# Top-k attention with a GELU block: reciprocals of the sums on POOL, and six more odd items turned by DVE and DRAM

## The chip, the cores and the metric

The kernel runs on one core of a Trainium2 chip. Its metric is the device time of one execution in microseconds (us); lower is better. Five engines work side by side, each through its own list of instructions in order, and they meet through semaphores: PE (matrix products, which also does transposes as products with an identity), DVE (vector work along a row), ACT (functions, and copies out of PSUM), POOL (vector work) and SP (which here only issues DMAs).

## The reference

There are 64 heads (batch 8 by 8 heads) with 576 rows and a head width of 64. For each head the scores are q times k transposed, times 1/8. In each row the 32 largest scores stay, a softmax is taken over those, and the result is multiplied with v. The outputs of the 8 heads of a batch are laid side by side into 512 columns, which gives 4608 rows, and these pass through two matrix products with an exact GELU between them.

```python
scores = scale * np.matmul(q, k.transpose(0, 1, 3, 2))
kth = np.partition(scores, -top_k, axis=-1)[..., -top_k:-top_k + 1]
scores = np.where(scores >= kth, scores, -1000000000.0)
attn = np.exp(scores - np.max(scores, axis=-1, keepdims=True))
attn = attn / (np.sum(attn, axis=-1, keepdims=True) + 1e-09)
x = bridge(np.matmul(attn, v))               # (4608, 512)
h = x @ w_in                                 # (4608, 2048)
out = (0.5 * h * (1.0 + erf(h / sqrt(2)))) @ w_out
```

## The kernel before

The work is cut into 144 items. An item is a tile of 128 rows for a pair of heads, and its tile `s` holds two rows of 576 scores side by side in each partition (128 x 1152). A batch has 18 items: 16 of full rows and two that collect the ends of the heads (64 rows each). Two batches make a round of 36 items (`RINGS`), and the program repeats with that period once the start is over.

The main loop (L1205) has one pass per item, here called slot n. All engines get their instructions in the order in which the loop writes them, so a slot is a stretch of each engine's list and not a stretch of time. What happens to item i, in order:

- Slot i-2: PE makes the scores (L408, and the last keys at L373), and ACT copies them to `s` (L416, L381). In slots of even number the scores of two items are made at once.
- End of slot i-2 to slot i-1: DVE takes the larger of the two halves of a row (L446, `larger`), and POOL their sum and then the smaller (L477, L485).
- Slot i: DVE finds the 32nd largest value of each row in `top_k` (eight MAX8 and six MATCH_REPLACE8). POOL then makes the threshold and the bias from it (L527, L528, `threshold`).
- Slot i+1: ACT pushes what is below the threshold far down (L547, `select`) and takes the exponential with the row's sum (L559, `softmax`). POOL adds 1e-9 to the sums (L540, `add_small`). At the end of `top_k` of that slot DVE takes the reciprocal of the two sums of each partition (L534, `inverse`), and POOL multiplies the tile with it (L582, `normalise`), behind the threshold of the next item.
- Slot i+2: the tile is turned so that keys lie along the partitions, in one of two ways. In the first, PE transposes it in nine pieces (one at L666, eight at L680) and ACT copies them from PSUM to the tile `pt` (L669, L695). In the second, DVE transposes squares of 32 x 32 in place (L614, `square_p`, in the middle of `top_k`), and SP writes the tile to DRAM (L624, `write_p`) and, a slot later, reads it back in another order into `pt` (L634, `read_p`).
- Slot i+3, when i is odd: PE multiplies `pt` of the items i-1 and i with v (L751, `attend`), ACT copies the result to `xT` (L756). `pt` exists once.

Which items take the second way is said by `squared`. These are, from item 27 on, nearly all items of even number, the items of ends, and those odd ones for which `moved` holds. An odd item that is moved has its product with v a slot later (slot i+4 in place of i+3), in the middle of the slot, with its own PSUM pair `pr`. The list `mid` in the main loop does that. `room_in` gives slot i+2 of such an item two pieces less of the matrix products of the second block, and slot i+3 two more.

The second block fills PE between these: first product (L820), GELU (L836), second product by seven products for eight (L974, L976), and the sums of it on POOL (L857 to L860, L997). In odd slots ACT copies one result of the second product out of PSUM (L995); the bank in which that result lies is the one into which PE next puts the last keys (L373).

`top_k` takes a function `last` that it calls behind the last MAX8: it issues `larger(n + 2)` and then `inverse(n - 1)`. A set `have_larger` keeps `larger` from being issued twice.

Of the kernel before, what the change touches and what calls it, by code (L numbers as in the profile page):

```python
# [14 lines left out]
def kernel(  # L15
# [19 lines left out]
    nc = tc.nc  # L35
    f32, i32, u32 = mybir.dt.float32, mybir.dt.int32, mybir.dt.uint32
    bf16, i16, u16 = mybir.dt.bfloat16, mybir.dt.int16, mybir.dt.uint16
    AF = mybir.ActivationFunctionType
    ALU = mybir.AluOpType

    B, H, S, D = q.shape
    P = 128
# [19 lines left out]
    const = ctx.enter_context(tc.tile_pool(name="const", bufs=1))  # L62
# [47 lines left out]
    def flush():  # L110
        held[0] = False
        while late_issues:
            late_issues.pop(0)()
        late_issues.extend(later)
        later.clear()
# [61 lines left out]
    DIAGS = START - 1  # L177
    SINGLE = range(18, 28)
    words = {}
    bounds = const.tile([P, 2], f32, name="bounds")  # L180
    low, high = bounds[:, 0:1], bounds[:, 1:2]
    nc.gpsimd.memset(low, -EXP0 * 2.0**20)
    nc.gpsimd.memset(high, EXP0 * 2.0**-40)

# [71 lines left out]
    for b in range(B):  # L258
# [4 lines left out]
        last = [(b * NP + p, NM) for p in range(0, NP, 2)]  # L263
# [8 lines left out]
    N = len(items)  # L272
# [4 lines left out]
    few = [False]  # L277
# [55 lines left out]
    S_of, stat_of = {}, {}  # L333
# [98 lines left out]
    def paired(i):  # L432

        return PAIRED <= i < N and i not in SINGLE

    def halves_of(i):
        s = S_of[i].rearrange("p (e h n) -> p e h n", e=2, h=2)
        return s[:, :, 0], s[:, :, 1]

    have_larger = set()  # L440

    def larger(i):

        if paired(i) and i not in have_larger:
            have_larger.add(i)
            nc.vector.tensor_tensor(lists_for(i)[:, :, 0], *halves_of(i), op=ALU.max)  # L446

    def into_of(i):

        if i < 2 and i not in into_lists:  # L450
            into_lists[i] = work.tile([P, 2, 2, HS], f32, tag="pt", bufs=1, name="into")
        return into_lists.get(i, lists_of[i])
# [13 lines left out]
    def lists_for(i):  # L466

        if i not in lists_of:
            lists_of[i] = work.tile([P, 2, 2, HS], f32, tag="lists", name="lists")
        return lists_of[i]  # L470
# [10 lines left out]
    def smaller(i):  # L481

        if paired(i):
            both, top = lists_of[i][:, :, 1].bitcast(i32), lists_of[i][:, :, 0].bitcast(i32)
            nc.gpsimd.tensor_tensor(into_of(i)[:, :, 1].bitcast(i32), both, top, op=ALU.subtract)  # L485

    def top_k(i, last, middle):


        stat_of[i] = st = {  # L490
            "first": work.tile([P, 2, 8], f32, tag="first", name="first"),
        }
        stat = work.tile([P, 4, 2], f32, tag="stat", name="stat")
        st.update((n, stat[:, x]) for x, n in enumerate(("neg", "bias", "den", "rden")))
        top = work.tile([P, 2, 16], f32, tag="top", bufs=1, name="top")
        into = [st["first"]] + [
            top[:, :, 8:16] if r == TOPK // 8 - 1 else top[:, :, 0:8] for r in range(1, TOPK // 8)
        ]
        if paired(i):
            t = lists_of[i]  # L500
            u = into_of(i)
            both = u.rearrange("p e h n -> p e (h n)")
            rounds = [(t[:, :, 0], u[:, :, 0]), (u[:, :, 0], u[:, :, 0])]
            rounds = [(*(rounds[r] if 16 * r < TOPK else (both, both)), x) for r, x in enumerate(into)]
        else:
            s = S_of[i].rearrange("p (e n) -> p e n", e=2)
            t = work.tile([P, 2, S], f32, tag="lists", name="rest")
            rounds = [(s if r == 0 else t, t, x) for r, x in enumerate(into)]
        for r, (src, dst, x) in enumerate(rounds):
            if 16 * r == TOPK:  # L510
                middle()
            for e in range(2):
                nc.vector.max(x[:, e], src[:, e])  # L513
            if r < len(rounds) - 1:
                for e in range(2):
                    nc.vector.match_replace(dst[:, e], x[:, e], src[:, e], LOWEST)  # L516
            if r == len(rounds) - 1:
                last()

        st["kth"] = top[:, :, 15]  # L520

    def threshold(i):

        if i < 0 or i >= N:
            return
        st = stat_of[i]
        nc.gpsimd.tensor_scalar(st["neg"], st["kth"], -1.0, None, op0=ALU.mult)  # L527
        nc.gpsimd.tensor_tensor(st["bias"], st["kth"], st["first"][:, :, 0], op=ALU.subtract)  # L528

    def inverse(i):  # L530
        if i < 0 or i >= N:
            return
        st = stat_of[i]
        nc.vector.reciprocal(st["rden"], st["den"])  # L534

    def add_small(i):
        if i < 0 or i >= N:
            return
        st = stat_of[i]
        nc.gpsimd.tensor_scalar(st["den"], st["den"], 1e-9, None, op0=ALU.add)  # L540

    def select(i, e):

        if i < 0 or i >= N:
            return
        st, s = stat_of[i], row(i, e)
        nc.scalar.activation(s, s, func=AF.Prelu, bias=st["neg"][:, e : e + 1], scale=1.0, alpha=STEEP)  # L547
        selected.add((i, e))
# [37 lines left out]
    def squared(i):  # L586

        if not SINGLE.stop - 2 < i < N - 2:
            return False
        if items[i][1] == NM:  # L590
            return i % RINGS != RINGS // 2 - 1
        return moved(i) or (i % 2 == 0 and i % RINGS != 12)

    LATER = (3, 13, 25, 31)

    def moved(i):

        return RINGS <= i < N - 8 and i % RINGS in LATER

# [10 lines left out]
    def square_p(i):  # L610

        if squared(i):
            s = S_of[i]
            nc.vector.transpose(s, s)  # L614

    def write_p(i):

        if squared(i):
            turned[i] = d = dram.tile([SQ, NJ + NM, P // SQ, P], f32, tag="turned", name="turned")
            s = S_of.pop(i).rearrange("p (x j) -> p x j", j=SQ)  # L620
            d = d.rearrange("i c k n -> i (c k) n")
            for a in range(P // SQ):
                rows = slice(a * SQ, (a + 1) * SQ)
                nc.sync.dma_start(out=d[:, :, rows], in_=s[rows])  # L624
# [498 lines left out]
    def mlp(n):  # L1123
        for _ in range(n):
            if done[0] >= len(pieces) or pieces[done[0]][0] > ready[0] or left[0] == 0:
                return
            pieces[done[0]][1]()
            done[0] += 1
            left[0] -= 1
            if eager[0]:  # L1130
                run_gelus()
                run_small(9)
# [72 lines left out]
    for n in range(ahead):  # L1205
# [27 lines left out]
        if n > 0:  # L1233
            larger(n + 1)
# [58 lines left out]
        if few[0]:  # L1293
            room = ODD if n % 2 else 0
            if mid and (mid[0] in starts_next or mid[0] % RINGS == LATER[0]):
                mlp(1)
# [34 lines left out]
            softmax(n - 1, 1)  # L1331
        if n > 0:
            smaller(n + 1)
        add_small(n - 1)
        for piece in tr[-1:] + prep:
            piece(None)
            mlp(1)
# [5 lines left out]
        mlp(left[0])  # L1343
        run_gelus()
        if n < N:
            def last():
                if few[0]:
                    larger(n + 2)
                inverse(n - 1)

            top_k(n, last, lambda: square_p(n - 2))
            write_p(n - 2)
            flush()
            if n == 0:
                larger(1)
        else:
            inverse(n - 1)
        threshold(n)
        if n == 0:
            smaller(1)  # L1360
# [60 lines left out]
```

## Time and profile before

| | |
|---|---|
| median of 3 runs | 1462.1 us (1461.39 to 1462.64) |
| the profiled execution | 1461.3 us, span 1459.5 us |
| PE busy | 1442.6 us, 99% of the span |
| DVE busy | 1329.6 us, 91% |
| POOL busy | 1128.4 us, 77% |
| ACT busy | 1056.4 us, 72% |
| DMA | mean 94 GB/s, 136.49 MB |

The span runs from the first instruction to the last. A row of a group of instructions has the line of the kernel, the engine, the operation, the tiles (out<-in), the shapes and the count; behind the bar stand the busy time of the group in us, the mean duration of one in ns, and the idle time of the engine just ahead of them with what ended it. Durations of matrix products overlap, since PE works on several at once. What one of them costs is therefore read from the start of one to the start of the next. PEld is the loading of PE's weights, which runs beside the products.

### The profile page before, as it was taken

The page shows a single profiled execution, that of the slowest core. Times are in us where ns is not written, and L with a number is a line of the kernel's source. Part 1 is how long each engine was busy: PE and PEld are TensorE (multiplying, and loading weights), DVE is VectorE, ACT ScalarE, POOL GpSimd, SP SyncE. Part 2 cuts the span into 40 slices and gives each one's busy share as a digit, 9 for nine tenths or more (in the row PEclk, how much of TensorE's full clock was granted, in tenths as well). Part 3 has the DMA queues.
Part 4 walks back from the last instruction along what each step waited for, and adds up shares of the span by engine and source line. Part 5 has one row for each costly group of instructions (what it writes and reads, how often), then busy time and mean ns, then how long its engine had stood idle before and what let it go on. Part 6 is the DMA issues. An engine that isn't in the chain of part 4 may idle for free.

```text
span 1459.5 us, 26550 instructions
## 1 busy us (share of the span) xinstructions
PE 1442.6 (99%) x8621; PEld 1123.9 (77%) x8621; DVE 1329.6 (91%) x3339; ACT 1056.4 (72%) x1883; POOL 1128.4 (77%) x1290
## 2 busy tenths in 40 slices
PE   8999999999999999999999999999999999999999
PEld 6776678877777777787777778787777777787887
DVE  7999999999999999999999999999999999999601
ACT  7999977777777777767777777777676767677620
POOL 6877657877798878878888878887788887878632
PEclk9999999999999999999999999999999999999999
DMA  7524310045454446456554365456554444543200
GB/s 196 150 87 126 84 48 1 9 98 104 90 113 89 87 87 142 82 113 128 111 99 96 65 117 116 90 112 127 117 102 106 90 80 84 127 98 85 53 15 15
DMA packets 591819, 136.49 MB, mean 94 GB/s; under 512 B 504352, under 2 KB 583232, under 8 KB 591680
## 3 DMA queue, kind: packets, MB, share of 16 engines
q1 hardware_dynamic: 590416, 134.37, 43.5%
q8 instruction: 68, 1.11, 0.3%
q14 instruction: 71, 0.58, 0.1%
q10 hardware_dynamic: 1200, 0.39, 0.1%
q0 software_dynamic: 64, 0.03, 0.0%
HBM read 85.19 MB, written 49.55 MB: 92 GB/s over the span
## 4 chain that ended last, share of the span: by engine, by line
PE 44%; POOL 11%; DVE 7%; issue 3%; ACT 3%; DMA 1%; SPq 0%; DVEq 0%; POOLq 0%; ACTq 0%
PE h_ps L820 17%; PE y_ps L976 11%; PE o L751 5%; PE s_ps L408 3%; POOL s L582 3%; DVE top L513 3%; DVE lists L516 2%; POOL lists L485 2%; POOL lists L477 2%; PE seven L974 2%; PE tp L680 2%; PE y_ps L938 2%; PE y_ps L941 1%; DMA turned<-s 1%; DVE s L614 1%
## 5 line engine op out<-in xcount | busy, mean ns | idle before, releaser
L820 PE MATMUL h_ps<-xT,w_in_sb 128*128 128x256 f32 (+1 forms) x2560 | 533.0, 361 | 0.0
L820 PEld LDWEIGHTS h_ps<-xT,w_in_sb 128*128 128x128 f32 x2560 | 438.9, 191 | 69.2 <-issue 10.9
L513 DVE MAX8 top<-lists 128x8 f32<-128x576 f32 (+1 forms) x792 | 475.9, 641 | 0.0
L547 ACT ACTIVATE s<-s,stat 128x576 f32<-128x576 f32 x288 | 219.2, 786 | 123.0 <-POOL stat L527 122.9
L516 DVE MATCH_REPLACE8 lists<-top,lists 128x288 f32<-128x288 f32 (+1 forms) x528 | 308.0, 589 | 0.0
L582 POOL TENSOR_TENSOR s<-s,stat 128x1152 f32<-128x1152 f32 x135 | 284.8, 2109 | 10.1 <-DVE stat L534 5.3
L559 ACT ACTIVATE s<-s,stat 128x576 f32<-128x576 f32 x288 | 225.2, 787 | 7.6
L485 POOL TENSOR_TENSOR lists<-lists 128x576 int32<-128x576 int32 x132 | 186.6, 1413 | 3.1
L477 POOL TENSOR_TENSOR lists<-s 128x576 int32<-128x576 int32 x133 | 188.2, 1415 | 0.0
L540 POOL TENSOR_SCALAR stat<-stat 128x2 f32<-128x2 f32 x144 | 44.4, 309 | 163.0 <-ACT s L559 156.1
L751 PE MATMUL o<-pt,raw_v 128*64 128x256 f32 x1280 | 152.9, 384 | 1.0 <-ACT pt L685 0.4
L416 ACT ACTIVATE s<-s_ps 128x1024 f32<-128x1024 f32 x127 | 126.4, 1046 | 35.2 <-PE s_ps L408 35.0
L751 PEld LDWEIGHTS o<-pt,raw_v 128*64 128x64 f32 x1280 | 86.8, 136 | 80.9 <-issue 38.1
L976 PE MATMUL y_ps<-w_out_sb,sum 128*128 128x256 f32 x472 | 140.4, 379 | 0.0
L408 PE MATMUL s_ps<-kt,qm 64*128 64x512 f32 x512 | 131.2, 621 | 1.1 <-ACT s L414 0.8
L836 ACT ACTIVATE g<-h_ps 128x512 f32<-128x512 f32 x144 | 78.2, 595 | 66.6 <-PE h_ps L820 66.0
L446 DVE TENSOR_TENSOR lists<-s 128x576 f32<-128x576 f32 x133 | 106.2, 799 | 17.8 <-ACT s L381 5.8
L976 PE MATMUL y_ps<-w_out_sb,g 128*128 128x256 f32 x480 | 116.4, 382 | 0.0
L516 DVE MATCH_REPLACE8 lists<-first,lists 128x288 f32<-128x288 f32 x264 | 114.4, 439 | 0.0
L513 DVE MAX8 first<-lists 128x8 f32<-128x288 f32 x268 | 105.8, 434 | 0.0
L976 PEld LDWEIGHTS y_ps<-w_out_sb,g 128*128 128x128 f32 x480 | 90.4, 190 | 15.0 <-issue 3.1
L976 PEld LDWEIGHTS y_ps<-w_out_sb,sum 128*128 128x128 f32 x472 | 89.8, 190 | 12.1
(162 smaller groups left out, 2359.0 us busy)
## 6 DMA issues: line engine op xcount, KB each, us to landing
turned<-s SPq DMA_DIRECT2D x272, 144.0 KB, 3.6
pt<-turned SPq DMA_DIRECT2D x272, 144.0 KB, 3.2
raw_v<-in_v_dram SPq DMA_DIRECT2D x64, 128.0 KB, 2.5
raw_q<-in_q_dram SPq DMA_DIRECT2D x112, 72.0 KB, 2.3
raw_k<-in_k_dram SPq DMA_DIRECT2D x112, 72.0 KB, 2.4
out_dram<-y SPq DMA_DIRECT2D x30, 256.0 KB, 3.1
w_out_sb<-in_moe_w_in_dram SPq DMA_DIRECT2D x14, 511.8 KB, 4.9
w_out_sb<-in_moe_w_out_dram SPq DMA_DIRECT2D x10, 511.8 KB, 4.1
```

Of the source, the lines that this page charges most:

```text
L408: nc.tensor.matmul(s_ps[:, e], lhsT=q_t[rows, :], rhs=kt[rows, main_keys(pair)], start=True, stop=True)
L416: nc.scalar.activation(spread(s, S + TL, SM), s_ps, func=AF.Copy, scale=scale)
L477: nc.gpsimd.tensor_tensor(t[:, :, 1].bitcast(i32), a.bitcast(i32), b.bitcast(i32), op=ALU.add)
L485: nc.gpsimd.tensor_tensor(into_of(i)[:, :, 1].bitcast(i32), both, top, op=ALU.subtract)
L513: nc.vector.max(x[:, e], src[:, e])
L516: nc.vector.match_replace(dst[:, e], x[:, e], src[:, e], LOWEST)
L547: nc.scalar.activation(s, s, func=AF.Prelu, bias=st["neg"][:, e : e + 1], scale=1.0, alpha=STEEP)
L559: nc.scalar.activation(s, s, func=AF.Exp, bias=st["bias"][:, e : e + 1], scale=1.0, accum_out=st["den"][:, e : e + 1],)
L582: nc.gpsimd.tensor_tensor(s, s, wide, op=ALU.mult)
L751: nc.tensor.matmul(o[e * D : (e + 1) * D, 0:n], lhsT=vt[:, j, e, :], rhs=pt[:, e * NJ + j if j < NM else NM, :], start=(j == 0), stop=(j = ...
L820: nc.tensor.matmul(h_tile(u)[:, i, :], lhsT=w_in_sb[:, ko, f * P : (f + 1) * P], rhs=xT[:, ko, c0 : c0 + n], start=(ko == 0), stop=(ko == ...
L976: nc.tensor.matmul(acc[names][:, k], lhsT=lhsT, rhs=rhs, start=(j == 0 and k == 0), stop=(j == FT // 2 - 1 and k == 1),)
```

## The change

The reciprocal leaves DVE. `inverse` now runs on POOL, takes in the addition of 1e-9 and raises the sum to the power -1 with a second small instruction, against a column of -1 that is set once. It is called where `add_small` stood, ahead of the threshold in POOL's list. `top_k` loses its argument `last`: `larger(n + 2)` isn't issued behind the last MAX8 any more but at the beginning of the next slot, as `larger(n + 1)` seen from there, which is the next thing in DVE's list all the same.

`LATER` gains the numbers 5 and 23. With the condition in `moved` (items 36 to 135) these are the items 41, 59, 77, 95, 113 and 131. They go from PE's transposes to DVE's squares with the way through DRAM, and their product with v moves from slot i+3 to the middle of slot i+4.

```diff
-    bounds = const.tile([P, 2], f32, name="bounds")
+    bounds = const.tile([P, 3], f32, name="bounds")
+    minus = bounds[:, 2:3]
...
+    nc.gpsimd.memset(minus, -1.0)
...
-    have_larger = set()
-
     def larger(i):
 
-        if paired(i) and i not in have_larger:
-            have_larger.add(i)
+        if paired(i):
             nc.vector.tensor_tensor(lists_for(i)[:, :, 0], *halves_of(i), op=ALU.max)
...
-    def top_k(i, last, middle):
+    def top_k(i, middle):
...
-            if r == len(rounds) - 1:
-                last()
...
         st = stat_of[i]
-        nc.vector.reciprocal(st["rden"], st["den"])
-
-    def add_small(i):
-        if i < 0 or i >= N:
-            return
-        st = stat_of[i]
         nc.gpsimd.tensor_scalar(st["den"], st["den"], 1e-9, None, op0=ALU.add)
+        nc.gpsimd.tensor_tensor(
+            st["rden"], st["den"],
+            bass.AP(tensor=minus.tensor, offset=minus.offset, ap=[list(minus.ap[0]), [0, 2]]),
+            op=ALU.pow,
+        )
...
-    LATER = (3, 13, 25, 31)
+    LATER = (3, 5, 13, 23, 25, 31)
...
-        add_small(n - 1)
+        inverse(n - 1)
...
-            def last():
-                if few[0]:
-                    larger(n + 2)
-                inverse(n - 1)
-
-            top_k(n, last, lambda: square_p(n - 2))
+            top_k(n, lambda: square_p(n - 2))
...
-        else:
-            inverse(n - 1)
```

## Prediction

> **What bounds the kernel now.** First the page: busy times, and DVE in 40 slices.
>
> ```profile
> PE 1442.6 (99%) x8621; PEld 1123.9 (77%) x8621; DVE 1329.6 (91%) x3339; ACT 1056.4 (72%) x1883; POOL 1128.4 (77%) x1290
> DVE  7999999999999999999999999999999999999601
> ```
>
> PE is busy throughout, and DVE nearly so until the last 80 us. The view by stretches shows both in the steady part (us, then busy time and instructions of PE, PEld, DVE, ACT, POOL). The first row is the start, the next two are rounds of 36 slots, the last is the tail.
>
> ```profile
> 0.00:111.40 111.40, 100.85 (x741) 79.89 (x743) 101.83 (x279) 99.62 (x171) 83.65 (x93) 1.00 0.49 142
> ...
> 695.80:1037.80 342.00, 341.01 (x2014) 266.06 (x2012) 332.98 (x839) 249.08 (x450) 283.51 (x323) 1.00 0.52 105
> 1037.80:1380.00 342.20, 341.54 (x2031) 266.90 (x2027) 325.95 (x827) 250.10 (x452) 282.37 (x324) 1.00 0.46 94
> 1380.00:1459.50 79.50, 75.66 (x368) 65.35 (x366) 4.90 (x12) 14.78 (x32) 23.65 (x33) 0.99 0.04 14
> ```
>
> A round takes 342.0 us, 9.5 per slot. PE is idle for 1.0 us of it, DVE for 9.0, POOL for 58.5, which is 1.62 per slot. That PE is truly full is read from starts (start, us, engine, line):
>
> ```profile
> 784.85 0.27 PE L666 MATMUL tp_t<-ident,s 128*128 128x128 f32 x1
> 784.96 0.60 PE L976 MATMUL y_ps<-w_sum,sum 128*128 128x256 f32 x2
> ...
> 785.82 1.04 PE L680 MATMUL tp<-ident,s 128*128 128x128 f32 x8
> 786.70 0.60 PE L976 MATMUL y_ps<-w_sum,g 128*128 128x256 f32 x2
> 787.13 0.59 PE L976 MATMUL y_ps<-w_out_sb,sum 128*128 128x256 f32 x2
> 787.66 1.99 PE L408 MATMUL s_ps<-kt,qm 64*128 64x512 f32 x8
> ```
>
> Two products of 256 columns take 0.43 us from start to start, and eight transposes of 128 columns 0.88: 0.9 ns per column both times, with no hole between kinds. The Trainium skill (Perfetto Trace Analysis, Identifying the Most-Contended Engine) says that matmul busy time is a poor measure of how full PE is, and asks for LDWEIGHTS busy time; that is 266 of 342 us here, and by that rule a fifth would be free and taking products away would be worth little. The starts above show no such room, and other rows show waits only at a few spots (below), so I keep PE as the bound and give the rule's outcome a place among the rivals.
>
> So PE sets the end, DVE has 3% of slack, and the two lean on each other through POOL and ACT.
>
> **The change part by part.** Rows of groups (busy us, mean ns | idle before), and of two small POOL instructions min/median/max ns:
>
> ```profile
> L680 PE MATMUL tp<-ident,s 128*128 128x128 f32 x536 | 69.6, 273 | 0.0
> L666 PE MATMUL tp_t<-ident,s 128*128 128x128 f32 x67 | 18.8, 281 | 0.0
> L695 ACT COPY pt<-tp 128x1024 f32<-128x1024 f32 x65 | 66.3, 1020 | 34.9 <-PE tp L680 34.6
> L669 ACT COPY pt<-tp_t 128x128 f32<-128x128 f32 x76 | 21.4, 282 | 4.2 <-PE tp_t L666 4.2
> L614 DVE STREAM_TRANSPOSE s<-s 128x1152 f32<-128x1152 f32 x68 | 92.8, 1365 | 0.0
> L534 DVE RECIPROCAL stat<-stat 128x2 f32<-128x2 f32 x144 | 22.7, 158 | 31.1 <-POOL stat L540 27.8
> L528 POOL TENSOR_TENSOR stat<-top,first 128x2 f32<-128x2 f32 x144 | 55.9, 388 | 0.0
> ...
> L540 POOL TENSOR_SCALAR stat<-stat x144: 217/218/833, 26.2 to 1381.8; 128x2 f32<-128x2 f32 x144
> L527 POOL TENSOR_SCALAR stat<-top x144: 218/218/1312, 18.2 to 1375.7; 128x2 f32<-128x2 f32 x144
> ```
>
> *PE, transposes away.* Six items lose nine transposes each: 0.88 + 0.11 (784.85 to 784.96) = 0.99 us, six times: **-5.9**. The two pieces that `room_in` moves between slots i+2 and i+3 are the same work.
>
> *PE, the product with v moved.* Before, it follows the scores directly. In its new place it stands alone between full-height products. A change of shape costs about 0.1 us (787.13 to 787.66 is 0.53, against 0.43 without one), and there is one such change more: 6 x 0.1 = **+0.6**.
>
> *ACT* loses 1.02 + 0.28 us per item, 7.8 in all. It is 72% busy: 0 on the path, and its relief comes behind the waits priced below.
>
> *DVE* loses 144 x 158 ns = 22.7 us and up to 31.1 us of waits for POOL's sum, and gains 6 x 1.365 = 8.2. The net is 14.5 or more off. DVE isn't the bound, so 0 directly; what it gives is an earlier end of `top_k`. `larger` keeps its place in DVE's list: 0, covered by the same neighbours.
>
> *DMA.* Each item adds four writes, four reads on SP's queue:
>
> ```profile
> turned<-s SPq DMA_DIRECT2D x272, 144.0 KB, 3.6
> pt<-turned SPq DMA_DIRECT2D x272, 144.0 KB, 3.2
> ```
>
> The 6.8 us from square to `pt` stand against the slot and a half, some 14 us, that the moved product leaves. Each read waits on SP for its write to land, and the loads and the next write queued behind it wait too, 3.6 us at most. Cost 0; if that cover is gone PE waits for `pt`.
>
> *POOL, the power.* No row has one. From below, a POOL instruction on 128x2 takes at least 0.217 us (L540's shortest); from above I use 1.31, the longest that one of this size took (L527's). Nearest is L528, also with two inputs of 128x2: mean 0.39. With 0.08 of hand-over from L540 to L527 (798.74 to 798.82 below) I take p = 0.47, ends 0.30 and 1.39. On average it is covered by the 1.62 us per slot of idle POOL. But it stands ahead of the threshold, and ACT waits for that, in one round:
>
> ```profile
> ACT s L547 <- POOL stat L527: 39.8, 13, 6.2
> POOL stat L540 <- ACT s L559: 33.4, 14, 4.3
> DVE stat L534 <- POOL stat L540: 3.5, 4, 1.0
> PEld s_ps L408 <- ACT pt L695: 2.7, 6, 0.9
> ```
>
> Behind the waiting ACT the chain goes on to PE. All engines, in slots 82 and 83:
>
> ```profile
> 797.90 0.77 DVE L446 TENSOR_TENSOR lists<-s 128x576 f32<-128x576 f32 x1
> 798.13 0.61 POOL L540 TENSOR_SCALAR stat<-stat 128x2 f32<-128x2 f32 x1
> ...
> 798.82 0.22 POOL L527 TENSOR_SCALAR stat<-top 128x2 f32<-128x2 f32 x1
> ...
> 799.07 1.44 ACT L547 ACTIVATE s<-s,stat 128x576 f32<-128x576 f32 x2 [3.80 <-POOL stat L527]
> ...
> 802.79 0.38 ACT L995 COPY p<-seven 128x256 f32<-128x256 f32 x1
> ...
> 803.43 0.39 PE L373 MATMUL tp_t<-kt,qm 128*128 128x128 f32 x2
> ```
>
> ACT selects, loads the GELU's table, runs two GELUs, and only then frees at 803.17 the bank that PE fills at 803.43: 0.26 us to spare. The same pair in slots 75, 79 and 97:
>
> ```profile
> 728.03 0.38 ACT L995 COPY p<-seven 128x256 f32<-128x256 f32 x1
> 728.66 0.38 PE L373 MATMUL tp_t<-kt,qm 128*128 128x128 f32 x2
> ...
> 765.28 0.38 ACT L995 COPY p<-seven 128x256 f32<-128x256 f32 x1
> 765.79 0.41 PE L373 MATMUL tp_t<-kt,qm 128*128 128x128 f32 x2
> ...
> 937.83 0.38 ACT L995 COPY p<-seven 128x256 f32<-128x256 f32 x1
> 938.26 0.49 PE L373 MATMUL tp_t<-kt,qm 128*128 128x128 f32 x2 [0.32 <-ACT p L995]
> ```
>
> Room of 0.25, 0.13 and none (PE waits already), mean of the four 0.16. These recur each round: 12 spots, 12 x (0.47 - 0.16) = 3.7 us if nothing comes earlier. Against that DVE's list is shorter by 0.16 us per slot and by its waits, so thresholds come earlier relative to PE; but POOL and not DVE is late in such slots (L540 begins 0.23 behind L446). I take half: **+1.8**, ends 0 and 12 x 1.23 = 14.8.
>
> The same rows show something else: L540 takes 0.61 beside L446 and ends 0.07 behind it, where its median is 0.22. The Trainium skill (SBUF — State Buffer, Who interferes with whom) states that a VectorE instruction with two SBUF inputs and a GpSimd one that reads SBUF exclude each other, the later one waiting; the trace agrees. By that rule a power that starts in L446's shadow costs up to 0.77 in place of 0.39, and one that starts ahead of L446 holds DVE up.
>
> *Start.* In the first slots POOL's multiplied diagonals come p later; ACT is the fuller engine there (99.62 of 111.40 us, with the loading of the first data in it) and I count 0. Without that cover it is about two slots, 0.9.
>
> Sum against the profiled execution: 1461.3 - 5.9 + 0.6 + 1.8 = 1457.8. That execution lies 0.8 below the median of the runs, so the forecast is **1458.6**, 3.5 us or 0.24% faster. A difference under 0.2% (2.9 us) is about what a measurement can't tell from none.
>
> **The rivals.**
>
> *B, no lateness.* DVE's freed time covers the power, and PE's idle time in the steady part (1.0 and 0.7 us in the rounds shown, another 0.7 taken for the first) goes too: 1458.6 - 1.8 - 2.4 = 1454.4. For it: DVE waited for POOL's sum (3.5 per round), and this ends. Against: POOL's own lateness.
>
> *C, the power's delay reaches PE (the slower side).* Place: the 12 spots. Price 12 x (p - 0.16) with no relief. The 5.3 us gained are gone at p = 0.60; slower by 0.2% from p = 0.84. With L540's longest, 0.83 + 0.08 = 0.91, it is 1462.1 - 5.3 + 9.0 = 1465.8. At p = 1.39: 1471.6. For it: ACT's 39.8 us of waits for L527. Against: a power as long as a multiplication.
>
> *D, a power far above all rows.* Beyond 1.62 us per slot POOL is the bound: at 3 us, 36 x 1.4 = 50 per round, three rounds: about 1610. No row speaks for it; none excludes it.
>
> *F, the squares make DVE late.* In slots 7 and 25 of a round DVE gets 1.37 longer just where PE gets shorter; two odd slots on, PE has 0.26 to spare. 6 x (1.37 - 0.26) = 6.7 eats the gain: 1462.1 - 5.3 + 6.7 = 1463.5. That is what the rule on matmul busy time comes to here: products taken off PE return as waits. Against: four reciprocals less (0.63) ahead of that spot.
>
> *E, the change doesn't do what it says:* `pt` comes late for the moved products, with waits of 0.9 us each (the 5.3 over six) the gain is lost: 1462.1.
>
> **How the numbers follow.** Forecast 0.45 (1456.5 to 1460.5), B 0.15, C 0.15, F 0.12, D 0.08, E 0.05. The range reaches down to B less the unpaid 0.6, 1453.5, and up to C at p = 0.91, 1466; outside stay D, C's upper part and a little of E. Faster by over 0.2% (below 1459.2): B and three quarters of the forecast, 0.5. Slower (above 1465): D, half of C, some of F: 0.2. Within: 0.3.
>
> **What would show it.** L680 x488, L666 x61, L614 x74, L534 gone, and a POOL row of 144 powers whose mean is p. ACT's wait for L527 grows by p in the slots with that wait; PE's waits at L373 for L995 tell C from B. If L446 waits for ACT more, DVE has run ahead. A power of over 1 us, or waits of PE behind the new squares, would make the forecast wrong.

## The result and the profile after

The changed kernel takes 1483.29 us (median, 1482.55 to 1483.7), the kernel before 1461.92 us beside it. The ratio is 1.0145 with a 95% interval of 1.013 to 1.0161: 21.4 us slower, where 3.5 us faster was forecast and 1466 was the upper end of the range.

First the page of the changed kernel: span, busy times, and POOL's 40 slices.

```profile
span 1481.8 us, 26751 instructions
PE 1446.2 (98%) x8567; PEld 1116.9 (75%) x8567; DVE 1340.7 (90%) x3201; ACT 1050.7 (71%) x1871; POOL 1219.1 (82%) x1435
POOL 6888668978898889888898989998888988988732
```

No engine is fuller than before except POOL, which went from 77% to 82%. A loss of 21 us with every share below 99% has to be sought in waits.

The groups that the change touches show that it was made as described (line, engine, operation, tiles, shapes, count; busy us, mean ns; idle before):

```profile
L676 PE MATMUL tp<-ident,s 128*128 128x128 f32 x488 | 63.7, 273 | 3.6 <-ACT xT L752 3.6
L610 DVE STREAM_TRANSPOSE s<-s 128x1152 f32<-128x1152 f32 x74 | 101.6, 1373 | 9.3 <-POOL s L578 9.3
L532 POOL TENSOR_TENSOR stat<-stat,bounds 128x2 f32<-128x2 f32 x144 | 108.1, 750 | 12.0
L531 POOL TENSOR_SCALAR stat<-stat 128x2 f32<-128x2 f32 x144 | 52.8, 367 | 151.8 <-ACT s L555 145.0
L445 DVE TENSOR_TENSOR lists<-s 128x576 f32<-128x576 f32 x133 | 122.1, 919 | 29.8 <-ACT s L383 18.2 <-ACT s L394 1.0
```

48 of the big transposes (and six of the small ones) have left PE, six squares have come to DVE, and the reciprocal is gone. The power (L532) takes 0.75 us in the mean and 0.72 in the median, with 12.0 / 144 = 0.08 us of hand-over ahead of it. `larger` is L445 now (L446 before). Its mean was 799 ns and is 919, with the same work.

The waits of the whole trace (who waited <- for whom; us, times, longest):

```profile
ACT s L543 <- POOL stat L524: 170.8, 54, 6.7
DVE lists L445 <- ACT s L383: 18.2, 23, 2.2
DVE top L512 <- POOL stat L525: 11.2, 16, 1.8
PE t_ps L375 <- ACT p L991: 10.4, 9, 1.6
PE tp_t L375 <- ACT p L991: 5.0, 10, 0.7
```

Before, the first of these was 122.9 us in 45 waits; DVE's wait for POOL's bias (L525, which must read the one buffer of `top` before the next MAX8 writes there) did not exist, and PE's waits for that copy came to 1.0 us in three. PE waits at the kind of spot that the forecast had looked at, the last keys (L375 now) for ACT's copy of the bank (L991). These two rows are 15.4 us; PE's time without work went from 16.9 us of the span to 35.6.

Stretches of four slots show where this comes from (us; busy time and instructions of PE, PEld, DVE, ACT, POOL). Three of them of the kernel before, and then, behind a whole round, the same slots of the changed kernel:

```profile
733.12:769.82 36.70, 36.66 (x195) 28.12 (x191) 36.07 (x93) 26.94 (x49) 34.21 (x40) 1.00 0.53 112
886.43:924.25 37.82, 37.56 (x315) 30.61 (x313) 36.28 (x93) 26.84 (x49) 34.10 (x41) 1.00 0.65 140
924.25:961.19 36.94, 36.62 (x224) 28.65 (x221) 36.28 (x93) 28.07 (x52) 30.93 (x36) 1.00 0.40 78
```

```profile
703.65:1052.90 349.25, 342.14 (x1999) 263.07 (x1998) 338.01 (x805) 247.02 (x446) 306.29 (x359) 1.00 0.55 109
742.13:781.01 38.88, 37.35 (x189) 27.20 (x186) 37.92 (x89) 27.51 (x49) 36.95 (x45) 1.00 0.54 104
898.78:937.51 38.73, 38.13 (x317) 30.72 (x315) 37.32 (x88) 27.43 (x51) 36.82 (x44) 1.00 0.64 135
937.51:976.83 39.32, 37.21 (x219) 27.97 (x216) 37.93 (x90) 26.34 (x50) 33.87 (x41) 1.00 0.52 103
```

The first row of the second fence is a whole round: 349.25 us against 342.0. Three rounds with some 7 us more each make nearly the whole loss. In the first stretch POOL had 36.70 - 34.21 = 2.49 us free over four slots, 0.62 per slot. The round's mean, on which the forecast leaned, was 1.62. Four powers with hand-over are 4 x 0.80 = 3.2 us: they do not fit, and the stretch has grown by 2.18 us.

The share over four slots doesn't tell the whole, though. The stretch that grew most, by 2.38 us, is the third, where POOL had 6.01 us free and still has 5.45; the first two together make 3.1 of the round's 7.2 us. Most of POOL's idle time is waiting for ACT and PE, and much of it stayed: over the round POOL got 22.8 us more to do, its idle time fell by only 15.5, and the round grew by 7.2. Taken slot by slot (from DVE's first MAX8 of one slot to that of the next), POOL had under 0.8 us free in 14 of the 36 slots, two of them, with 0.24 each, in the third stretch. Why the growth lies behind some of these slots and not behind others isn't settled: another stretch, in which POOL had 5.63 us free, got 1.03 us shorter.

One slot of the first stretch from POOL to PE, first before, then after (start, us, engine, line; other rows are left out, and the forecast showed the last two steps of before):

```profile
759.15 1.42 POOL L485 TENSOR_TENSOR lists<-lists 128x576 int32<-128x576 int32 x1
760.65 0.22 POOL L540 TENSOR_SCALAR stat<-stat 128x2 f32<-128x2 f32 x1
760.69 0.76 DVE L446 TENSOR_TENSOR lists<-s 128x576 f32<-128x576 f32 x1
760.95 0.58 POOL L527 TENSOR_SCALAR stat<-top 128x2 f32<-128x2 f32 x1
761.56 1.44 ACT L547 ACTIVATE s<-s,stat 128x576 f32<-128x576 f32 x2 [6.15 <-POOL stat L527]
```

```profile
769.42 1.41 POOL L484 TENSOR_TENSOR lists<-lists 128x576 int32<-128x576 int32 x1
770.12 1.32 DVE L445 TENSOR_TENSOR lists<-s 128x576 f32<-128x576 f32 x1
770.92 0.61 POOL L531 TENSOR_SCALAR stat<-stat 128x2 f32<-128x2 f32 x1
771.61 0.71 POOL L532 TENSOR_TENSOR stat<-stat,bounds 128x2 f32<-128x2 f32 x1
772.29 0.23 POOL L524 TENSOR_SCALAR stat<-top 128x2 f32<-128x2 f32 x1
772.56 1.44 ACT L543 ACTIVATE s<-s,stat 128x576 f32<-128x576 f32 x2 [6.74 <-POOL stat L524]
...
776.28 0.38 ACT L991 COPY p<-seven 128x256 f32<-128x256 f32 x1
776.72 0.49 PE L375 MATMUL t_ps<-kt,qm 128*128 128x128 f32 x2 [1.39 <-ACT p L991]
```

From the start of POOL's last big instruction (L485, now L484) to ACT's select went 2.41 us before and 3.14 after, 0.73 more. The room in this slot was 0.13 us by the forecast; a wait of 1.39 needs 1.52, so about 0.8 us of lateness had been brought along from the slots before, where POOL was full too. The rows show a second thing. `larger` now starts while POOL's L484 runs, takes 1.32 in place of 0.76 and ends at 771.44, 0.61 behind L484's end.

### The profile page after: what moved, and what is told of

Its sections match the earlier page's. It is cut to its first block, busy times and chain, and to the rows that moved or that the text cites. A ratio compares the mean times of both kernels' runs of the same rounds, so it can differ in the third digit from the quotient of the medians.

```text
span 1481.8 us, 26751 instructions
## 1 busy us (share of the span) xinstructions
PE 1446.2 (98%) x8567; PEld 1116.9 (75%) x8567; DVE 1340.7 (90%) x3201; ACT 1050.7 (71%) x1871; POOL 1219.1 (82%) x1435
## 4 chain that ended last, share of the span: by engine, by line
PE 62%; POOL 15%; ACT 10%; DVE 5%; issue 3%; DMA 2%; SPq 1%; ACTq 0%; DVEq 0%; POOLq 0%
PE h_ps L816 23%; PE y_ps L972 12%; PE o L747 6%; PE s_ps L410 5%; PE tp L676 3%; POOL s L578 3%; ACT s L543 2%; DVE top L512 2%; POOL lists L484 2%; PE y_ps L934 2%; PE y_ps L916 2%; PE seven L970 2%; PE y_ps L937 2%; POOL lists L476 2%; ACT L832 2%
## 5 line engine op out<-in xcount | busy, mean ns | idle before, releaser
L484 POOL TENSOR_TENSOR lists<-lists 128x576 int32<-128x576 int32 x132 | 190.6, 1444 | 3.1
L531 POOL TENSOR_SCALAR stat<-stat 128x2 f32<-128x2 f32 x144 | 52.8, 367 | 151.8 <-ACT s L555 145.0
L445 DVE TENSOR_TENSOR lists<-s 128x576 f32<-128x576 f32 x133 | 122.1, 919 | 29.8 <-ACT s L383 18.2
L532 POOL TENSOR_TENSOR stat<-stat,bounds 128x2 f32<-128x2 f32 x144 | 108.1, 750 | 12.0
L610 DVE STREAM_TRANSPOSE s<-s 128x1152 f32<-128x1152 f32 x74 | 101.6, 1373 | 9.3 <-POOL s L578 9.3
```

## The experiments

The theory at first: the power stands ahead of the threshold, so every threshold is late by it (rival C of the forecast). Rivals: POOL's time counts wherever it stands; the six items are the loss (rival F); the freed DVE time is what does harm; the power, which reads two inputs from SBUF, holds up DVE's `larger`. The first four runs take the change apart. All times are medians in us, beside 1461.8 to 1461.9 for the kernel before.

**The power alone.** `LATER` stays as before.

```diff
-    LATER = (3, 5, 13, 23, 25, 31)
+    LATER = (3, 13, 25, 31)
```

> The changed kernel with LATER as before (3, 13, 25, 31): only the reciprocal's move is left. Theory 1 (the power, 0.72 us with its hand-over 0.08, stands ahead of the threshold and delays it, then ACT's selection, then PE at L373): the whole loss is here, and the six items give back some 5 us of PE's transposes; expects 1483 to 1489 us. Theory 2 (the six squares make DVE late, the power is mostly covered): expects 1463 to 1468 us.

Measured 1479.38, ratio 1.012 (1.0105 to 1.0135): 17.5 us. The power by itself makes most of the loss, and the wait of PE at the last keys is there without the items:

```profile
PE tp_t L375 <- ACT p L991: 12.2, 16, 1.6
```

**The items alone.** The kernel before with the new `LATER`.

> The kernel before with LATER as changed (3, 5, 13, 23, 25, 31): the reciprocal stays on DVE, the six items go by squares and DRAM. Theory 1: faster than before by up to the 5.3 us of the forecast's PE terms, 1457 to 1461 us. Theory 2: most of the loss is here, 1475 us or more. A third way: DVE, which keeps the reciprocals, has no room for 8.2 us of squares, and the time stays within 2 us of 1462.

Measured 1467.97, ratio 1.0042 (1.0027 to 1.0056): 6.1 us slower, where the transposes taken off PE should have given 5.3. A round of this kernel, and two of its waits:

```profile
697.96:1042.24 344.28, 340.88 (x1998) 263.55 (x1996) 335.77 (x841) 246.96 (x446) 283.10 (x323) 1.00 0.56 111
```

```profile
PE tp L680 <- ACT xT L756: 3.7, 6, 1.0
PE o L751 <- DMA pt<-turned: 1.1, 1, 1.1
```

The round is 2.3 us longer than before. DVE's busy time rose from 333.0 to 335.8, which is the two squares of 1.37, while its idle time stayed at 8.5 us (9.0 before): the round grew by about what DVE had to do more. PE's idle time rose from 1.0 to 3.4 us; the work taken off it came back as waits, in the next odd slot behind the square (L373 and L680) and once for `pt`. The first row is a cost of the moved product itself. Its result lies in the one PSUM pair into which PE next puts the transposes (both take it by `pair_tile`), and these wait until ACT has copied the result (L756): 0.98 us behind each of the three new items of number 5, and 0.25 behind the three old ones of number 25. In the kernel before, PE has no such wait. That PE's busy time did not fall in spite of 18 transposes less is not resolved further by the trace.

**A multiplication in place of the power**, in the changed kernel.

```diff
-            op=ALU.pow,
+            op=ALU.mult,
```

> The changed kernel with a multiplication in place of the power, on the same operands and in the same place: POOL's list, the waits and the six items are those of the changed kernel, only the length of that instruction falls, from 0.72 to about 0.2 us. It leaves the reciprocal out. Theory 1 expects the loss to go with the length: 1457 to 1463 us. Theory 2 expects 1475 us or more. If the place of one more POOL instruction counts, whatever its length, it stays above 1470.

Measured 1466.3, ratio 1.0031 (1.0019 to 1.0043). The 17 us between this kernel and the changed one hang on what the second instruction takes on POOL, 0.26 us or 0.75 in the mean. They don't hang on `larger`:

```profile
L445 DVE TENSOR_TENSOR lists<-s 128x576 f32<-128x576 f32 x133 | 124.1, 934 | 21.9 <-ACT s L383 7.8 <-ACT s L394 2.5 <-DVE top L512 0.5
```

Its mean is 934 ns with the multiplication and 919 with the power, so a power that holds up `larger` isn't where the 17 us come from.

**The power behind the threshold**, called between the threshold of item n and the normalisation of item n-1.

```diff
         nc.gpsimd.tensor_scalar(st["den"], st["den"], 1e-9, None, op0=ALU.add)
+
+    def power(i):
...
         nc.gpsimd.tensor_tensor(
             st["rden"], st["den"],
...
+        power(n - 1)
         normalise(n - 1)
```

> The changed kernel with the power behind the threshold and the bias of the next item, just ahead of the normalisation; the addition of 1e-9 stays in its place. POOL's work is the same. Theory 1 (what counts is what stands ahead of the threshold): most of the loss goes, 1458 to 1468 us, less what a later normalisation costs. A rival to it (POOL as a whole is too full, 0.8 us more per slot wherever it stands): within 4 us of 1483.

Measured 1483.49, ratio 1.015 (1.0133 to 1.0167), the same as the changed kernel. So the place ahead of the threshold isn't the cause, and the first theory fell. POOL's list in this run:

```profile
769.67 0.22 POOL L524 TENSOR_SCALAR stat<-top 128x2 f32<-128x2 f32 x1
769.86 0.20 POOL L525 TENSOR_TENSOR stat<-top,first 128x2 f32<-128x2 f32 x1
770.01 0.72 POOL L537 TENSOR_TENSOR stat<-stat,bounds 128x2 f32<-128x2 f32 x1
770.80 2.11 POOL L583 TENSOR_TENSOR s<-s,stat 128x1152 f32<-128x1152 f32 x1
```

The threshold is out before the power, but normalisation and everything behind it start later by the power, and so does the next threshold: in a full stretch POOL hands the delay on.

**Less of other work on POOL**, with the power alone (the first experiment), in 16 slots per round one difference of 0.73 us less.

```diff
-        add(a21, a11, a21, op=ALU.subtract)
+        if u == NU - 2:
+            add(a21, a11, a21, op=ALU.subtract)
```

> The power-only kernel (LATER as before) without one of the four sums that POOL makes for the seven products (the difference a11 - a21, 0.73 us, 16 times in a round): it leaves that difference out. POOL is relieved by 11.7 of the some 29 us per round that the power brought, while the power stays where it is. Theory A expects a third to two thirds of the loss to go, 1466 to 1473 us. Theory B expects 1477 to 1480.

Measured 1464.0, ratio 1.0014 (1.0005 to 1.0024): 15.4 of the 17.5 us come back, with the power still in its place and as long as before. What counts is POOL's time, whichever instruction takes it.

**No addition of 1e-9**, in the changed kernel: POOL is relieved by one small instruction per item. The sum holds the exponential of the largest value, so it is at least 1, and 1e-9 is less than half a last place of it.

```diff
-        nc.gpsimd.tensor_scalar(st["den"], st["den"], 1e-9, None, op0=ALU.add)
```

> The changed kernel without the addition of 1e-9 (the sum holds an exponential of 0, so it is at least 1 and the addition changes no bit of it): POOL is relieved by 0.22 us and a hand-over of 0.08 per slot, the power stays. If POOL's slack ends between 0.6 and 0.8 us, most of the 21 us goes, 1464 to 1472 us. If the power's own reading is the cause, 1478 to 1483.

Measured 1468.27, ratio 1.0044 (1.0029 to 1.0059). An instruction whose median is 0.22 us and mean 0.37 brings 15.0 us, since it goes from a full POOL. It also ran beside `larger` often, as the slot above shows (0.61 in place of 0.22).

**No reciprocal**, in the kernel before and with the new items. This separates DVE's relief from POOL's load.

```diff
-        nc.vector.reciprocal(st["rden"], st["den"])
```

> The kernel before without any reciprocal, as in the run of the items without it: LATER as before, normalisation multiplies with the sums, which leaves the reciprocal out. It shows the most that the reciprocal's move can bring. If PE alone is the bound, as forecast, 1461 to 1462 us. If DVE bounds as much as PE does, 1452 to 1458.

> The kernel with the six items alone (1468.0) without any reciprocal: normalisation multiplies with the sums themselves, which leaves the reciprocal out. DVE loses 144 small instructions and its waits for POOL's sums, POOL's list is that of before. If the items cost because DVE is full (its list longer by 2.7 us per round, the round by 2.3), the time falls to 1456 to 1463. If they cost at fixed places (the copy of the moved product, the reload of pt), it stays at 1465 to 1468.

Measured 1463.75 without the reciprocal, ratio 1.0013 (1.0004 to 1.0022), and 1464.34 with the items beside it, ratio 1.0017 (1.0008 to 1.0027). Taking 22.7 us of busy time from DVE makes the kernel 1.8 us slower when nothing else is changed. `larger` in one round, before and then without the reciprocal:

```profile
L446 DVE TENSOR_TENSOR lists<-s 128x576 f32<-128x576 f32 x36 | 28.7, 796 | 4.4 <-ACT s L381 0.8
```

```profile
L446 DVE TENSOR_TENSOR lists<-s 128x576 f32<-128x576 f32 x36 | 33.4, 928 | 5.8 <-ACT s L381 2.2 <-ACT s L392 0.5
```

DVE comes to `larger` earlier and meets a large instruction of POOL more often: 9 of 36 take over 0.9 us (eight beside L485, one beside the normalisation), where 3 did. This gives back 4.7 us per round. The reciprocal itself was worth less than its 158 ns: outside such meetings the step from the start of `larger` to that of the next MAX8 got shorter by 0.08 to 0.10 us. That the meetings are the whole of the 1.8 us is argued, not shown by a run. With the items there, the reciprocal's removal does help: 1467.97 without it removed, 1464.34 with, which falls between the two readings that the expectation had set apart. So the items cost 6.1 us with the reciprocal on DVE and 0.6 without it.

**Memsets and multiplications where the power stood**, with the old items, the reciprocal left out and the sum itself taken by the normalisation: how much POOL time costs how much, and whether the power does anything else.

```diff
-        nc.gpsimd.tensor_tensor(
-            st["rden"], st["den"],
-            bass.AP(tensor=minus.tensor, offset=minus.offset, ap=[list(minus.ap[0]), [0, 2]]),
-            op=ALU.pow,
-        )
+        for x in range(9):
+            nc.gpsimd.memset(bounds[:, 2 + x % 6 : 3 + x % 6], -1.0)
```

This is the run with nine. Six and 22 differ in the number, and the run with multiplications has this in place of the memsets:

```diff
+        for x in range(4):
+            nc.gpsimd.tensor_tensor(bounds[:, 6:8], bounds[:, 2:4], bounds[:, 4:6], op=ALU.mult)
```

> The power-only kernel (LATER as before) with six memsets of one column each in place of the power: POOL is held for about 0.6 us at the same place, by instructions that read nothing. It leaves the reciprocal out. Theory A (POOL is full over stretches of slots, and its time is passed on wherever it stands): most of the loss stays, 1472 to 1478 us. Theory B (the power reads two operands from SBUF and bars DVE's L445, whose mean went from 796 to 941 ns in a round): the loss goes, 1458 to 1465 us, and L445 falls back to about 0.80.

> The run with six memsets, with nine: POOL is held at that place for some 0.88 us, a little more than the power's 0.72 and its hand-over, still without reading anything. It leaves the reciprocal out. If POOL's time is what counts and its slack ends between 0.6 and 0.8 us per slot, the time jumps to that of the power, 1475 to 1483 us. If the power's reading of SBUF counts, it grows only by the 0.3 us more in the same measure as the six did (some 2 us for 0.6), 1467 to 1469.

> The reciprocal left out, the sum itself used by the normalisation, and 22 memsets of one column on POOL where the power stood (so the output is not normalised by the reciprocal). They read nothing from SBUF. From start to start a memset takes some 0.03 us, so that they should hold POOL for about 0.7 us longer than before, as the power does. Theory 'POOL's time alone': nine of them (0.32 us) cost 3.6 over the kernel without a reciprocal, 11 us per us of hold, so 0.7 us gives 1463.8 + 8 = 1471.5, up to 1474 at 14 per us; a bend upwards towards the power's 1479.4 may come as POOL's stretches fill. Rival 'the power does something else (it reads SBUF, or keeps the read ports)': 1467 to 1469, as with nine.

> The reciprocal left out, the sum itself used by the normalisation, and four multiplications of 128x2 on POOL where the power stood, each with two inputs in SBUF. From start to start such an instruction takes about 0.17 us (782.45, 782.63 and 782.78 in the run with six memsets), so POOL is held for about 0.7 us longer, as by 22 memsets, but with reading. 'POOL's time alone': the same as the 22 memsets within 1.5 us if the hold is the same. 'Reading counts': 3 us or more above the memsets, towards 1479.

Measured: six 1466.1, ratio 1.0029 (1.0017 to 1.0041); nine 1467.37, 1.0038 (1.0024 to 1.0053); 22 memsets 1474.23, 1.0086 (1.007 to 1.0103); four multiplications 1502.35, 1.0279 (1.0264 to 1.0294). The expectations for six and nine had taken a memset at its duration of 0.1 us. They overlap. A row of each number, from POOL's lists of three runs:

```profile
790.11 0.24 POOL L533 MEMSET bounds<- 128x1 f32 x6
```

```profile
782.21 0.33 POOL L533 MEMSET bounds<- 128x1 f32 x9
```

```profile
794.21 0.69 POOL L533 MEMSET bounds<- 128x1 f32 x22
794.86 0.22 POOL L524 TENSOR_SCALAR stat<-top 128x2 f32<-128x2 f32 x1
```

Each further one takes 0.03 us, so that nine are far from a power and 22 come near it. The multiplications missed their aim as well. All four write the same two columns, and each started 0.27 or 0.28 us behind the one before (798.07, 798.34, 798.62 and 798.89 in one slot), not 0.17 as expected, so that they held POOL for much longer than 22 memsets. To put all on one scale I took from each trace, over 106 or 107 slots of the steady part, the mean time from the start of the addition to the start of the threshold, without the threshold's own waits:

| in the power's place | addition to threshold, us | more than with nothing | time, us | loss | loss per us of hold |
|---|---|---|---|---|---|
| nothing | 0.38 | | 1463.75 | | |
| six memsets | 0.62 | 0.24 | 1466.1 | 2.4 | 10 |
| nine memsets | 0.69 | 0.30 | 1467.4 | 3.6 | 12 |
| 22 memsets | 1.08 | 0.69 | 1474.2 | 10.5 | 15 |
| the power | 1.22 | 0.84 | 1479.4 | 15.6 | 19 |
| four multiplications | 1.63 | 1.25 | 1502.4 | 38.6 | 31 |

The points lie on one curve that bends upwards, memsets that read nothing from SBUF and instructions that read two inputs alike, and the power lies on it. So POOL's time is enough as the cause, and the power needs no further effect. That reading from SBUF adds something small isn't excluded, since no two of them held POOL equally long. The bend is what one expects of an engine that is full in more and more slots: 144 slots would make 144 us per us if it were full in all.

**No addition in the kernel before**, and with the new items: POOL relieved, nothing else changed.

> The kernel before without the addition of 1e-9, which changes no bit of the sums: the reciprocal on DVE waits for ACT's sum directly. POOL's list is shorter by 0.3 us per slot and doesn't stop for ACT ahead of the threshold. If POOL's fullness costs already in the kernel before (L485 beside L446, thresholds late by up to 1.3 us), 1455 to 1460 us; if PE is the bound, as forecast, 1461 to 1462.

> The six items without the power (1468.0) and without the addition of 1e-9. If POOL's slack lets the items' gain through, 1456 to 1463 us. If the items cost because DVE's list is longer by 2.7 us per round, they stay some 4 to 6 us above the same kernel without them.

Measured 1458.15, ratio 0.9974 (0.9963 to 0.9985), which beats both kernels, and 1462.02, ratio 1.0002 (0.9992 to 1.0011). So the items cost 3.9 us here too. In the second run PE's waits at L680 for ACT's copy of the moved product are 5.7 us in six, 0.98 behind number 5 as with the addition and 0.92 behind number 25. A round of the first:

```profile
694.32:1035.90 341.58, 340.62 (x2016) 266.10 (x2014) 332.99 (x840) 249.26 (x450) 278.98 (x287) 1.00 0.53 105
```

POOL's free time rises from 58.5 to 62.6 us. The round is 0.45 us shorter, and it begins 1.5 us earlier, so the gain is spread over the kernel. PE has 1.0 us idle per round as before. The reciprocal on DVE, too, no longer waits for POOL (27.8 us of such waits before), and how much of the 3.8 us is owed to that isn't separated. The 3.8 us are far from the 15.0 that the same instruction was worth in the changed kernel, where POOL was full.

## Why the prediction was wrong

Four kernels make the path from before to after in steps: 1461.9; items added and reciprocal gone 1464.3; a second small instruction on POOL (the multiplication) 1466.3; that instruction a power 1483.3. The steps are 2.4, 2.0 and 17.0 us, all upwards.

- **PE, transposes away, -5.9, and the product moved, +0.6: not paid out.** The counts were right, but the items by themselves cost 6.1 us in place of giving 5.3. The +0.6 priced a change of shape and left out the PSUM pair: the transposes behind the moved product waited for ACT's copy of it, 3.7 us in all in the run with the items alone. Rival F expected the waits at the last keys two odd slots behind the square, with 0.26 us to spare; they came one odd slot behind it, at the last keys and at that copy. F's outcome, a loss of the gain, was right in kind, and its place was not.
- **"DVE isn't the bound, so 0": this step failed for the items.** DVE had 9.0 us idle in a round and PE 1.0, which I read as a ranking. But more work didn't fill DVE's idle time, and the round followed DVE's work: 2 x 1.37 = 2.7 more per round against 2.3 more measured. Without the reciprocal on DVE the items cost 0.6 us in place of 6.1. The 0.98 us behind each item of number 5 stayed in that run, so they don't come from the reciprocal's time on DVE. How the rest of the 6.1 is shared isn't separated by a run. The Trainium skill's rule (Perfetto Trace Analysis, Identifying the Most-Contended Engine), by which products taken off PE would be worth little, had the right outcome. The reason that the trace shows is another: PE's starts had no holes before, and holes came behind the squares and the moved products, where PE waited for ACT.
- **DVE's relief, 14.5 us or more off, counted as 0.** Taken alone, the reciprocal's removal cost 1.8 us, and `larger` met L485 more often; that this is the whole reason is argued. With the items there it gave 3.6 us. Items and relief together are the 2.4 us of the first step above, where 5.3 off were forecast.
- **`larger` "0, covered by the same neighbours": wrong.** The neighbours in DVE's list were the same, the one on POOL was not. But the same lengthening stands in runs of 1464 to 1466 us, so it isn't what cost most. I had quoted the rule on two SBUF inputs (the Trainium skill, SBUF — State Buffer, Who interferes with whom) for the power, and the power wasn't the partner in this round. The partner was L484, with 1.41 us and two SBUF inputs: `larger` ended 0.61 or 0.62 behind it in each of the nine long cases of the changed kernel's round. The rule holds in eight of them; in the ninth `larger` had begun 0.01 us earlier and still ended last. I applied it to the new instruction only and not to the pairs that its delay shifts against each other.
- **The power, 0.47 taken of 0.30 to 1.39: it measured 0.80**, 0.72 (median) and 0.08 of hand-over, inside the bounds. From the nearest row in shape I took too little. The lower end was misread as well: L528, of the same size, has a shortest of 0.185 us, below the 0.217 that I took as the least. By rival C's formula, 12 x (0.80 - 0.16) = 7.7 us, and by it the kernel would have come to 1464.5.
- **"On average it is covered by the 1.62 us per slot of idle POOL": the step that cost most.** The mean hid stretches with 0.62 per slot, which a view by four slots shows, and 14 slots of 36 with less than the 0.80 that the power takes; and the idle time elsewhere was waiting that the power filled only in part. Lateness then adds up over slots. The sum counted each spot as if POOL started it on time, 12 spots with one p each, and the upper end 12 x 1.23 = 14.8 us had the same flaw. The power alone cost 17.5 at p = 0.80. Measured by hold time, it was 19 us per us and bending upwards, not 12.
- **"It stands ahead of the threshold": true and without effect.** Behind the threshold it cost the same.
- **DMA and `pt`, 0:** nearly right, one wait of 1.1 us in the run with the items alone.
- **What would show it:** the text named powers of over 1 us, or waits of PE behind the new squares, as what would break the forecast. The second came. The first was not needed: 0.72 did it.

Rival C came nearest: its place (L375 for L991) was right, and its price was not. D's condition, 1.62 us per slot, was the mean again; the kernel showed its effect in part from about half of that.

## What to carry to other kernels

Before giving an engine a new instruction per step, cut the steady part into short stretches, down to single steps, and take the engine's idle time in the fullest of them: there the load must fit, not on average. In stretches of four steps a full step can still hide, as here behind 6.01 us of idle time. An engine at 77% whose results all others wait for can be worth more than one at 99%; here leaving out 0.3 us per item on POOL gave 3.8 us, and 0.8 us more took 17.5. When an engine is freed, look at which large instruction of a neighbour it will now run beside. When a product is moved, look at whose buffer it takes and who must empty it before the next user.

## What the runs showed of the hardware

- A power of 128x2 elements on POOL takes 0.72 us, where a multiplication with the same operands has a median of 0.195 us.
- Memsets of one column on POOL take 0.1 us each, but a further one behind others only 0.03.
- Four small multiplications on POOL that write the same place started 0.28 us apart; two small instructions that write different places started 0.18 apart (L524, L525 in the same run, median). That the place is the reason isn't shown.
- DVE's `larger`, with two SBUF inputs, ended 0.61 or 0.62 us behind the end of POOL's L484, also with two, where the two overlapped. That held even where it had begun 0.01 us earlier (730.52 and 730.53 in the changed kernel): it then took 2.04 us in place of 0.76.
- DVE's reciprocal of 128x2, 158 ns long, freed only 0.08 to 0.10 us from the start of `larger` to the next MAX8.
